# Batch 2's keys: cast by their loads and turned by DMA instead of by the matrix engine

## The chip, the cores and the metric

The kernel runs on one core of a Trainium2 chip. The metric is the device time of one execution in microseconds (us); the kernel before takes 355.89 us (median of 3 runs, 355.85 to 356.45). Five engines with queues of their own work beside each other: PE (TensorE, matrix products; its weight loads have a row PEld), DVE (VectorE), ACT (ScalarE), POOL (GpSimd) and SP (SyncE, which here only starts transfers). ACT and POOL start transfers too. Each engine takes its instructions in the order of the program and waits where data or a buffer is missing.

## What is computed

Causal attention with a decay bias, and a gated feed-forward block on its result:

```python
scores = scale * np.matmul(q, k.transpose(0, 1, 3, 2))        # 8 batches, 8 heads, 576 x 64
s_pos = np.maximum(s, 0.0)
cum = np.cumsum(s_pos, axis=-1)
bias = -(cum[:, :, :, None] - cum[:, :, None, :])
scores = np.where(causal, -1000000000.0, scores + np.minimum(bias, 0.0))
attn = softmax(scores)
x = np.matmul(attn, v).transpose(0, 2, 1, 3).reshape(4608, 512)
xn = x / rms(x) * rms_g
g = xn @ w_gate
out = (g * sigmoid(g) * (xn @ w_val)) @ w_out                 # 512 -> 1536 -> 512
```

## The kernel before

**Two jobs woven into one.** The feed-forward block runs over nine chunks of 512 tokens (`ffn(c)`, line 936). A chunk has 12 pairs of a gate group (line 946, four matmuls of 512 columns) and a value group (line 955, four more), and then four blocks of output matmuls (line 972). Between such groups `step()` (line 851) puts in what the attention needs next. A call of `step` is a slot; a chunk has 36 slots, 24 beside the gate and value groups and 12 beside the output blocks. Slot 0 is the start of chunk 0, so chunk 1 begins behind slot 36, slot 44 follows the fourth value group of chunk 1, slot 45 its fifth gate group. What `step` may put in a slot is decided while the program is written out, by counts of slots (`ready(lag, ...)`), not by time. The order of each engine's queue is fixed by it.

**How queries and keys reach PE.** The scores need queries and keys with the head's elements along the partitions, so each is cast from fp32 to bf16 (`kqn`) and turned (`kqT`). Three constants say which way a batch goes: from batch `XB = 2` on the queries are turned by DMA; from batch `KB = 3` on the keys are cast by the load itself (`load_k`, line 168, one transfer on POOL's queue for each of five blocks of rows) and turned by DMA; from batch `MB = 3` on the scores are computed in a wider form (`s_run`). `kq_dma` (line 178) starts one turning transfer on SP's queue, for one of five column blocks c of the queries (w = 1) or of the keys (w = 0); `x_seq` lists those to come, and a slot starts at most one, at least two slots behind the last.

**Batch 2 before the change.** Its queries come that way. Its keys are loaded in fp32 to `kq32` by ACT's queue (`load2(ACT, 0)`, slot 24, 1 MB and a tail of 128 KB), cast in five pieces on ACT (three) and POOL (two) in slots 36 to 38, turned by PE in four steps of four matmuls (`t_step`, line 199, slots 40 to 43) and a tail of four (`tail_step`, line 222, slot 56), each step read out of the matrix engine's memory by ACT (lines 211 and 235). The queries' five casts lie on ACT (two) and POOL (three) in slots 33 to 36, and their five turns start in slots 37, 39, 42, 44 and 46.

**What uses them.** `s_step(2, kb, g)` (line 257) computes the scores of key block kb for half g of the heads. It needs the keys' block kb and the queries' blocks kb and kb + 1. `av_step` multiplies the softmax weights with the values; x is scaled (`x_scale`, line 481, DVE) and turned to `xnT` by DMA (`xt_dma`, line 489, SP) or, for some blocks, by PE (`xt_step`, line 499).

**Checks.** `check` (line 573) puts on DVE, for every batch's queries and keys, one pass that takes magnitudes (`check_mag`, line 515) and two that keep a running maximum (`check_max`, line 520); their sum decides at the end whether the fast path was allowed.

Of the kernel before, what the change touches and what calls it, by code (L numbers as in the profile page):

```python
# [26 lines left out]
def kernel(  # L27
# [12 lines left out]
    nc = tc.nc  # L40
    B, H, S, D = q.shape
    DM = H * D
# [4 lines left out]
    NSC = 5  # L47
# [33 lines left out]
    kqTn = kqT.rearrange("d a w (h n) -> d a w h n", h=HP)  # L81
    kqTx = kqT.rearrange("d a w (c h n) -> d a w c h n", c=NSC, h=HP)
    XB = 2
    KB = 3
    MB = 3
    PERIOD, PACE, MLAG, XLAG, SQLAG = 9, 2, 1, 6, 2
    v_sb = mp.tile([128, 2, NSC, H, NV], BF16, name="v_sb")
# [437 lines left out]


    SLOTS = 36
    K2 = 33
    slot = [0]
    first, chunk = [0], [0]  # L530
    done = {}
# [17 lines left out]
    x_seq = []  # L549
# [5 lines left out]
    def ready(lag, *key):  # L555
        return at(*key) + lag <= slot[0]
# [16 lines left out]
    def check(b, ws=(1, 0)):  # L573
        t = slot[0] + (8 if b >= KB else 0)

        def when(w):
            if b < 2:
                return slot[0] % 2 and chunk[0] == b and slot[0] > 16
            return phase() >= 25 and slot[0] >= t and (w == 0 or ready(0, "cast", b, 1))
        dve_side.extend((lambda w=w: when(w), f) for w in (ws if b < KB else (0, 1)) for f in (  # L580
            lambda w=w: check_mag(b, w), lambda: check_max(0), lambda: check_max(1),
            lambda w=w: done.__setitem__(("check", b, w), slot[0]))[slice(None) if b < MB - 1 else slice(0, 2)]
            + (() if b < MB - 1 else (lambda w=w: (check_max(1), done.__setitem__(("check", b, w), slot[0])),)))
# [5 lines left out]
    def loads(b, w, when, lag):  # L589

        def main():
            load_kq(nc.scalar, b, w)
            last["L"] = slot[0]
            last["P"] = slot[0] + 2

        def tail():
            load_kq_tail(nc.scalar, b, w)
            done["raw", b, w] = last["L"] = slot[0]
        n = len(act_side)
        when(act_side, lag, [main, tail])  # L600
        act_side[n:] = [(lambda c=c: c() and slot[0] - last["L"] >= 3, f) for c, f in act_side[n:]]

    def casts(b):

        def key(c):
            load_k(b, c)
            last["P"] = slot[0]
            done["K", b, c] = slot[0]  # L610
            if c == NSC - 1:
                check(b)

        def over(w):
            done["cast", b, w] = slot[0]
            if w == 1 and b >= KB:
                if b + 2 < B:
                    loads(b + 2, 1, early, 28 if b <= KB + 1 else 4)
            elif b + 1 < KB or w == 1:
                loads(b + 1, w, early, 11 if (b, w) == (2, 0) else 4)  # L620
            else:
                loads(b + 2, 1, early, 12)
            if w == 1:
                x_seq.extend((b, ww, c) for c in range(NSC) for ww in ((1, 0) if b >= KB else (1,)))
            else:
                done["cast", b] = slot[0]
                check(b)

        def free(w):
            return ready(0, "check", b - 2, w) and (  # L630
                ready(0, "T", b - 2) if w == 0 and b < KB + 2 else
                b < XB + 2 or ready(4, "X", b - 2, w, 4))
        if b > 4:
            key_side.extend((lambda: free(0) and (slot[0] > 72 if b == KB + 1 else ready(0, "R", b - 2, 3) and slot[0] > 3 * SLOTS + 1) and slot[0] - last["P"] >= PACE, lambda c=c: key(c)) for c in range(NSC))
        fns = [(1, lambda r=r: cast_x(nc.gpsimd, b, 1, r)) for r in range(NSC)]
        if b == 2:
            fns[-1] = (1, lambda: (cast_x(nc.gpsimd, b, 1, NSC - 1), over(1)))
        else:
            fns += [(1, lambda: over(1))]
        if b > 4:  # L640
            act_cast.extend((lambda: ready(7, "raw", b, 1) and free(1), f) for f in
                            [lambda r=r: cast_x(nc.scalar, b, 1, r) for r in range(NSC)] + [lambda: over(1)])
            return
        if b < KB:
            fns += [(0, lambda r=r: cast(nc.gpsimd, b, 0, r, r + 1)) for r in range(NSC)]
            fns += [(0, lambda: over(0))]
        if b == 2:

            def put2(queue, t, *fs):
                queue.extend((lambda: slot[0] >= t and free(0) and free(1), f) for f in fs)  # L650
            put2(act_side, K2, *[lambda r=r: cast_x(nc.scalar, b, 1, r) for r in (3, 4)])
            put2(act_side, K2 + 3, *[lambda r=r: cast(nc.scalar, b, 0, r, r + 1) for r in (0, 1, 2)])
            put2(pool_side, K2, *[lambda r=r: cast_x(nc.gpsimd, b, 1, r) for r in (0, 1)],
                 lambda: (cast_x(nc.gpsimd, b, 1, 2), over(1)),
                 lambda: cast(nc.gpsimd, b, 0, 3, 4), lambda: (cast(nc.gpsimd, b, 0, 4, 5), over(0)))
            return
        pool_side.extend((lambda w=w: ready(7, "raw", b, w) and free(w) and (b < 4 or slot[0] > 67), f) for w, f in fns)
        if b <= 4 and b >= KB:
            key_side.extend((lambda c=c: free(0) and slot[0] > (44 if c < 2 else (b - 1) * SLOTS - 3) and slot[0] - last["P"] >= PACE, lambda c=c: key(c)) for c in range(NSC))
# [60 lines left out]

    def soon(b, qb):

        return (b, qb) == (KB, 2)

    def sq_lag(b, qb):
        return 1 if soon(b, qb) else SQLAG
# [42 lines left out]
        return (ready(2, "cast", b) or ready(2, "cast", b, w)) and (b < 2 or ready(1, "S", b - 2, 4, 0))  # L769

    def period(b):
        return 8 if b == KB else PERIOD

    def run_ready():
        if not s_seq or s_seq[0][0] < MB:
# [8 lines left out]
    def can_s():  # L784
        if not s_seq:
            return False
        b, kb, g = s_seq[0]
        if not slot_free(1 if b < MB else 2) or exp_q:
            return False
        if b >= MB:  # L790
            if slot[0] - last["S"] < 3 or slot[0] - last["run"] < period(b) or slot[0] - max(last[x] for x in ("AVT", "TT")) < 2:
                return False
            return run_ready()
        if b == 1 and (phase() < 24 and phase() % 2 == 0 or kb == 4 and at("AV", 1, 3, 1) > slot[0]):
            return False
        due = SLOTS * ((b * S + kb * 128) // DM) - (26 if b == 1 else 15 if b == 2 else 14)
        if slot[0] - last["S"] < (4 if slot[0] < due - 24 else 3 if slot[0] < due else 2):
            return False
        if b >= XB:
            return all(ready(5, "X", b, 1, c) for c in (kb, min(kb + 1, 4))) and (  # L800
                ready(5, "X", b, 0, kb) if b >= KB else ready(3, "T", b) if kb >= 3 else
                all(ready(4 if b == 2 else 3, "T", b, hp, 0) for hp in (2 * g, 2 * g + 1)))
        if kb >= 3 and not ready(3, "T", b):
            return False
        if kb == 4:
            return True
        return all(ready(3, "T", b, 2 * g + j, w) for j in (0, 1) for w in (0, 1))
# [43 lines left out]
    def step(bare=False, tanh=False):  # L851
# [11 lines left out]
        moved = False  # L863
        if scaled[0] < len(x_list):
            b, qb = x_list[scaled[0]]
            if ready(5 if (b, qb) == (1, 1) else (3 if soon(b, qb) else 5 if b == KB else XLAG) if b >= MB else 3, "AV", b, qb, 1):
                x_scale(b, qb)
                last["XS"] = slot[0]
                scaled[0] += 1
                if not by_pe(b, qb):  # L870
                    assert xt_seq[0] == (b, qb)
                    xt_dma(*xt_seq.pop(0))
                    done["XT", b, qb] = slot[0] + 4
                    moved = True
# [4 lines left out]
        if not moved and x_seq and slot[0] - last["X"] >= 2 and not (  # L879
                scaled[0] < len(x_list) and x_list[scaled[0]] != (1, 4) and ready(1 if x_list[scaled[0]][0] < MB else XLAG - 2, "AV", *x_list[scaled[0]], 1)):  # L880
            b, w, c = x_seq[0]
            old = ("R", b - 2, c) if b - 2 >= (XB if w else KB) else ("S", b - 2, 4, 0)
            if (ready(1 if b == 2 else 2, "cast", b, 1) and ready(1, *old)
                    and (w == 1 or ready(7, "K", b, c))):
                x_seq.pop(0)
                kq_dma(b, w, c)
                done["X", b, w, c] = last["X"] = slot[0]
                if b >= KB and (w, c) == (0, NSC - 1) and b + 2 < B:
                    casts(b + 2)
# [176 lines left out]
    with tc.manual_schedule():  # L1066
# [155 lines left out]
        def put(queue, n, *fns):  # L1222
            queue.extend((lambda: slot[0] >= n, f) for f in fns)
# [12 lines left out]
        put(v_side, 11, lambda: (load_wout(0), load_wout(6)))  # L1236
        later(v_side, 0, [
            lambda: load_v(1, 2), lambda: load_v(1, 3), lambda: load_v(1, 4), lambda: load2(POOL, 1)])
        put(act_side, 24, lambda: load2(ACT, 0))
        put(act_side, 30, lambda: nc.scalar.activation(out=vwx, in_=biasK[:, :, MB * H:BH], func=AF.Exp))  # L1240

        check(0, (0,))
# [202 lines left out]
```

## Time and profile before

| | |
|---|---|
| time, median of 3 runs | 355.89 us |
| time of the profiled execution | 355.58 us |
| its span on the core | 354.1 us |
| granted clock of TensorE | 0.999 |
| start of chunk 0, chunk 1, chunk 2 | 26.44, 67.26, 105.24 us |

Times in the views count from the start of the span; the profiled execution has 1.5 us outside it. A row of a timeline gives its start, how long it took, the engine (SPq and ACTq are queues that start transfers), the line of the kernel, the operation with output and inputs, the shape, and a count where like instructions in a row are merged. Matmuls overlap, so that what a group of them costs is read from the start of the next group, not from the duration in the row. In brackets stands the idle time before and what ended it.

### The profile page before, as it was taken

To read this page: it belongs to the slowest core of one execution; us is meant where nothing else is said; L and a number is where in the kernel's file an instruction comes from. 1 tells how busy PE (TensorE), PEld (TensorE's weight loads), DVE (VectorE), ACT (ScalarE), POOL (GpSimd) and SP (SyncE) were. 2 spreads that over 40 slices of the span, in tenths; PEclk is the share of its full clock that TensorE was granted. 3 is DMA by queue.
4 is the path that set the end of the run, shared out by engine and by line. 5 is a ranking of instruction groups with operands and counts; after the bars stand their busy time and mean duration, and the time that the engine had idled before them with its cause. 6 is when DMAs were issued, how large, how long until landed. Compare 5 with 4: busy or idle time off the path is not lost.

```text
span 354.1 us, 6889 instructions
## 1 busy us (share of the span) xinstructions
PE 340.6 (96%) x2374; PEld 165.3 (47%) x2419; DVE 276.9 (78%) x524; ACT 213.4 (60%) x471; POOL 204.5 (58%) x337
## 2 busy tenths in 40 slices
PE   5989999999999999999999999999999999999995
PEld 2445444544444444444554454444544554444443
DVE  6697989598967887798889887988798659836840
ACT  3988885878786546855677557654565445224321
POOL 6969754456769986687597987597745310000000
PEclk9999999999999999999999999999999999999999
DMA  7999999999969998999899999495510121020002
GB/s 220 142 213 270 180 175 259 181 211 181 98 123 177 146 179 118 233 141 202 143 170 105 117 131 185 46 113 90 143 29 17 57 94 23 0 91 30 0 34 93
DMA packets 130528, 45.68 MB, mean 129 GB/s; under 512 B 110548, under 2 KB 125656, under 8 KB 130488
## 3 DMA queue, kind: packets, MB, share of 16 engines
q0 software_dynamic: 67056, 13.70, 50.5%
q1 hardware_dynamic: 53792, 24.20, 33.3%
q10 hardware_dynamic: 9640, 7.29, 8.2%
q8 instruction: 20, 0.33, 0.4%
q14 instruction: 20, 0.16, 0.2%
HBM read 37.90 MB, written 9.44 MB: 134 GB/s over the span
## 4 chain that ended last, share of the span: by engine, by line
PE 77%; DVE 8%; POOL 4%; issue 4%; DMA 3%; ACT 2%; SPq 0%; DVEq 0%; POOLq 0%; ACTq 0%
PE psF L972 25%; PE psF L955 21%; PE psF L946 20%; DVE U L958 2%; PE psAV L443 2%; DMA kq<-in_q_dram 2%; DMA kqT<-kqn 2%; PE psS L286 2%; DVE Ht L951 1%; PE psAV L437 1%; DVE x_sb L453 1%; PE psF L367 1%; POOL v_sb L409 1%; POOL v_sb L194 1%; PE psS L367 1%
## 5 line engine op out<-in xcount | busy, mean ns | idle before, releaser
L955 PE MATMUL psF<-xnT,wv_sb 128*128 128x512 bf16 x424 | 109.9, 379 | 0.4
L946 PE MATMUL psF<-xnT,wg_sb 128*128 128x512 bf16 x414 | 109.0, 379 | 1.3 <-ACT xnT L511 0.3
L949 ACT ACTIVATE T<-psF 128x512 f32<-128x512 f32 x108 | 64.6, 598 | 62.9 <-PE psF L946 58.8
L972 PE MATMUL psF<-wout_sb,Ht 128*128 128x512 bf16 (+2 forms) x428 | 98.9, 373 | 1.4 <-issue 0.8
L958 DVE SCALAR_TENSOR_TENSOR U<-T,psF 128x512 bf16<-128x512 f32 x108 | 73.7, 682 | 24.1 <-ACT T L949 23.9
L951 DVE TENSOR_TENSOR Ht<-U,psF 128x512 bf16<-128x512 bf16 x99 | 67.8, 685 | 6.9
L972 PEld LDWEIGHTS <-Ht 128*128 128x128 bf16 x444 | 40.1, 98 | 43.5 <-issue 1.4
L955 PEld LDWEIGHTS <-wv_sb 128*128 128x128 bf16 x432 | 39.6, 98 | 44.5 <-issue 2.9
L946 PEld LDWEIGHTS <-wg_sb 128*128 128x128 bf16 x432 | 39.4, 98 | 42.9 <-issue 2.4
L976 ACT ACTIVATE osb<-psF 128x512 f32<-128x512 f32 (+2 forms) x37 | 21.7, 587 | 58.4 <-PE psF L972 50.8
L384 POOL TENSOR_SCALAR_AFFINE_SELECT E<-E 128x512 bf16<-128x512 bf16 (+1 forms) x50 | 34.8, 704 | 28.5 <-ACT E L380 18.7
L194 POOL DMA_DIRECT2D v_sb<-in_v_dram x40 | 35.3, 885 | 0.2 <-issue 0.2
L484 DVE SCALAR_TENSOR_TENSOR xs_sb<-x_sb,al_all,g_row 128x512 bf16<-128x512 bf16 (+1 forms) x36 | 29.6, 823 | 4.1 <-POOL al_all L477 3.9
L474 POOL TENSOR_SCALAR al_all<-ss_all 128x1 f32<-128x1 f32 (+2 forms) x39 | 11.5, 295 | 35.9 <-ACT xs_sb L461 27.9
L310 ACT ACTIVATE E<-psS,biasK 128x256 bf16<-128x256 f32 (+3 forms) x88 | 29.2, 426 | 2.6 <-PE psS L286 2.6
L453 DVE TENSOR_TENSOR x_sb<-psAV,rZ 128x256 bf16<-128x256 f32 (+1 forms) x66 | 28.0, 424 | 2.3
L522 DVE TENSOR_TENSOR acc<-acc,mag 128x1280 bf16<-128x1280 bf16 x32 | 27.3, 873 | 0.2
L477 POOL TENSOR_TENSOR al_all<-al_all,mhalf 128x1 f32<-128x1 f32 (+2 forms) x39 | 25.2, 645 | 3.2
L443 PEld LDWEIGHTS <-E 128*128 128x128 bf16 x320 | 21.7, 97 | 10.5 <-POOL E L384 0.7
L461 ACT ACTIVATE xs_sb<-x_sb 128x512 bf16<-128x512 bf16 (+1 forms) x37 | 23.3, 629 | 4.6 <-DVE x_sb L453 4.0
L409 POOL TENSOR_TENSOR v_sb<-v_sb,vwx 128x512 bf16<-128x512 bf16 x25 | 25.9, 1037 | 0.1
L443 PE MATMUL psAV<-v_sb,E 128*128 128x65 bf16 x264 | 23.8, 193 | 0.1
(136 smaller groups left out, 379.8 us busy)
## 6 DMA issues: line engine op xcount, KB each, us to landing
out_dram<-osb SPq DMA_DIRECT2D x35, 256.0 KB, 2.7
kq<-in_q_dram ACTq DMA_DIRECT2D x5, 1024.0 KB, 7.5
v_sb<-in_v_dram POOLq DMA_DIRECT2D x32, 128.0 KB, 4.9
kqn<-in_k_dram POOLq DMA_DIRECT2D x20, 128.0 KB, 5.1
kq<-in_k_dram SPq DMA_DIRECT2D x4, 512.0 KB, 5.8
kq<-in_q_dram SPq DMA_DIRECT2D x4, 512.0 KB, 7.5
wout_sb<-in_moe_w_out_dram POOLq DMA_DIRECT2D x2, 768.0 KB, 10.5
kq<-in_q_dram POOLq DMA_DIRECT2D x1, 1024.0 KB, 11.0
```

Source lines behind the costliest of these rows:

```text
L194: nc.gpsimd.dma_start(out=v_sb[0:n, b % 2, c, :, 0:64], in_=v[b, :, c * 128:c * 128 + n, :].rearrange("h p d -> p h d"))
L384: nc.gpsimd.affine_select(out=Ev, in_=Ev, pattern=[[0, 4], [1, nq]], compare_op=ALU.is_ge, fill=0.0, base=0, channel_multiplier=-1)
L409: nc.gpsimd.tensor_tensor(out=v_sb[:, b % 2, c, :, 0:64], in0=v_sb[:, b % 2, c, :, 0:64], in1=vwx[:, c, i:i + H].unsqueeze(2).to_broadcast ...
L443: nc.tensor.matmul(o, lhsT=d, rhs=v_sb[:, p, qb, h, :], start=(j == 0 and qb == 0), stop=(j == 3))
L453: nc.vector.tensor_tensor(out=xo[:, g * 256:(g + 1) * 256].rearrange("p (h d) -> p h d", h=4), in0=pv[R, :, 0:64], in1=rZ[R].unsqueeze(2). ...
L484: nc.vector.scalar_tensor_tensor(out=xs_sb[R, (b * NSC + qb) % NX, :], in0=x_sb[R, (b * NSC + qb) % NX, :], scalar=al_all[R, col:col + 1], ...
L946: nc.tensor.matmul(Gp, lhsT=wg_sb[:, cc, fs], rhs=xnT[:, cc, x0:x0 + DM], start=(cc == 0), stop=(cc == CC - 1))
L949: nc.scalar.activation(out=T, in_=Gp, func=AF.Tanh, scale=0.5)
L951: nc.vector.tensor_tensor(out=Ht[:, fb - 1, :], in0=pend[0], in1=pend[1], op=ALU.mult)
L955: nc.tensor.matmul(Vp, lhsT=wv_sb[:, cc, fs], rhs=xnT[:, cc, x0:x0 + DM], start=(cc == 0), stop=(cc == CC - 1))
L958: nc.vector.scalar_tensor_tensor(out=U, in0=T, scalar=1.0, in1=Gp, op0=ALU.add, op1=ALU.mult)
L972: nc.tensor.matmul(Op[:, p0:p1], lhsT=Ht[:, fb, tb * 128:(tb + 1) * 128], rhs=wout_sb[:, fb, p0:p1], start=(fb == 0), stop=(fb == FB - 1))
```

## The change

The constant `KB` goes from 3 to 2. With it batch 2's keys are loaded and cast by POOL's queue in five transfers (slots 24, 26, 36, 43 and 45, by the list `K0`) and turned by five DMA transfers on SP (slots 33, 35, 44, 50 and 56). The fp32 load of the keys on ACT's queue, their five casts, PE's 20 transposing matmuls and the five copies out of the matrix engine's memory fall away. Of the queries' casts three now lie on ACT and two on POOL. `x_seq` for batch 2 is written out by hand, keys and queries mixed. The queries' turns start in slots 37, 39, 42, 46 and 52 instead of 37, 39, 42, 44 and 46. The scores of batch 2 start in slot 44 instead of 45, and several of its later steps one or two slots earlier. The checks of batch 1's queries start in slot 35, at the end of chunk 0, instead of slot 37. Conditions that named `KB` for what begins at batch 3 now name `MB`. From slot 73 on both programs have the same order.

```diff
-    KB = 3
+    KB = 2
...
-    K2 = 33
+    K2, K0 = 33, (24, 26, 36, 39, 42)
...
             if b < 2:
-                return slot[0] % 2 and chunk[0] == b and slot[0] > 16
+                return slot[0] % 2 and (16 < slot[0] < SLOTS if b == 0 else slot[0] > 34 and slot[0] - last["XS"] > 1)
...
             if w == 1 and b >= KB:
+                if b == KB:
+                    loads(3, 1, early, 4)
                 if b + 2 < B:
-                    loads(b + 2, 1, early, 28 if b <= KB + 1 else 4)
-            elif b + 1 < KB or w == 1:
-                loads(b + 1, w, early, 11 if (b, w) == (2, 0) else 4)
-            else:
-                loads(b + 2, 1, early, 12)
-            if w == 1:
+                    loads(b + 2, 1, early, 14 if b == KB else 28 if b <= KB + 2 else 4)
+            elif b + 1 < KB:
+                loads(b + 1, w, early, 4)
+            if w == 1 and b > 2:
                 x_seq.extend((b, ww, c) for c in range(NSC) for ww in ((1, 0) if b >= KB else (1,)))
-            else:
+            elif w == 0:
                 done["cast", b] = slot[0]
                 check(b)
...
-            put2(act_side, K2, *[lambda r=r: cast_x(nc.scalar, b, 1, r) for r in (3, 4)])
-            put2(act_side, K2 + 3, *[lambda r=r: cast(nc.scalar, b, 0, r, r + 1) for r in (0, 1, 2)])
-            put2(pool_side, K2, *[lambda r=r: cast_x(nc.gpsimd, b, 1, r) for r in (0, 1)],
-                 lambda: (cast_x(nc.gpsimd, b, 1, 2), over(1)),
-                 lambda: cast(nc.gpsimd, b, 0, 3, 4), lambda: (cast(nc.gpsimd, b, 0, 4, 5), over(0)))
+            put2(act_side, K2, *[lambda r=r: cast_x(nc.scalar, b, 1, r) for r in (3, 4)],
+                 lambda: (cast_x(nc.scalar, b, 1, 2), over(1)))
+            put2(pool_side, K2, *[lambda r=r: cast_x(nc.gpsimd, b, 1, r) for r in (0, 1)])
+            key_side.extend((lambda c=c: free(0) and slot[0] >= K0[c] and slot[0] - last["P"] >= PACE, lambda c=c: key(c)) for c in range(NSC))
+            x_seq.extend([(2, 0, 0), (2, 0, 1), (2, 1, 0), (2, 1, 1), (2, 1, 2), (2, 0, 2), (2, 1, 3), (2, 0, 3), (2, 1, 4), (2, 0, 4)])
             return
...
-        return (b, qb) == (KB, 2)
+        return (b, qb) == (MB, 2)
...
-        return 8 if b == KB else PERIOD
+        return 8 if b == MB else PERIOD
...
-        due = SLOTS * ((b * S + kb * 128) // DM) - (26 if b == 1 else 15 if b == 2 else 14)
+        due = SLOTS * ((b * S + kb * 128) // DM) - (26 if b == 1 else 13 if (b, kb) == (2, 2) else 15 if b == 2 else 14)
...
-            if ready(5 if (b, qb) == (1, 1) else (3 if soon(b, qb) else 5 if b == KB else XLAG) if b >= MB else 3, "AV", b, qb, 1):
+            if ready(5 if (b, qb) == (1, 1) else (3 if soon(b, qb) else 5 if b == MB else XLAG) if b >= MB else 3, "AV", b, qb, 1):
...
-            if (ready(1 if b == 2 else 2, "cast", b, 1) and ready(1, *old)
+            if ((ready(1, "cast", b, 1) or w == 0) if b == 2 else ready(2, "cast", b, 1)) and (ready(1, *old)
                     and (w == 1 or ready(7, "K", b, c))):
...
-        put(act_side, 24, lambda: load2(ACT, 0))
```

## The prediction

> **What bounds the kernel now.** First the top of the profile's page, then what PE waited for from 26 us, where the chunks begin, to 130 us (second fence) and from there to the end (third).
>
> ```profile
> span 354.1 us, 6889 instructions
> PE 340.6 (96%) x2374; PEld 165.3 (47%) x2419; DVE 276.9 (78%) x524; ACT 213.4 (60%) x471; POOL 204.5 (58%) x337
> ```
> ```profile
> PE psF L946 <- ACT xnT L511: 0.3, 1, 0.3
> ```
> ```profile
> PE psF L972 <- issue: 0.8, 5, 0.2
> ```
>
> PE is busy for 96% of the span, and behind 26 us it waits 0.3 + 0.8 = 1.1 us in all. So the time is the sum of what PE is given: one us less of matmuls is one us less of time, and one us of new waiting is one more. ACT and POOL have 40% of the span free; their work counts only where it makes something late for PE.
>
> **What PE no longer does.** Below are rows of PE's timeline in chunk 1, the first and the last of the four transposing steps of batch 2's keys and what stands around them, and then the tail.
>
> ```profile
> 70.96 0.39 PE L203 MATMUL psAV<-ident_bf,kqn 128*128 128x128 bf16 x4
> 71.18 1.03 PE L946 MATMUL psF<-xnT,wg_sb 128*128 128x512 bf16 x3
> ...
> 74.22 0.39 PE L203 MATMUL psAV<-ident_bf,kqn 128*128 128x128 bf16 x4
> 74.44 1.03 PE L955 MATMUL psF<-xnT,wv_sb 128*128 128x512 bf16 x4
> 75.30 1.03 PE L946 MATMUL psF<-xnT,wg_sb 128*128 128x512 bf16 x4
> 76.26 0.39 PE L286 MATMUL psS<-kqT 64*128 64x256 bf16 x4
> ...
> 81.34 0.29 PE L443 MATMUL psAV<-v_sb,E 128*128 128x65 bf16 x4
> 81.47 1.02 PE L946 MATMUL psF<-xnT,wg_sb 128*128 128x512 bf16 x4
> 82.43 0.39 PE L286 MATMUL psS<-kqT 64*128 64x256 bf16 x4
> ```
> ```profile
> 87.88 0.39 PE L228 MATMUL psT<-ident_bf,kqn 128*128 128x128 bf16 x4
> 88.10 1.03 PE L946 MATMUL psF<-xnT,wg_sb 128*128 128x512 bf16 x3
> ```
>
> A step's row says 0.39 us, but the next group starts 71.18 - 70.96 = 0.22 us later, and it is starts that add up on a full engine. Four steps are 4 x 0.22 = 0.89 us with the last digits (0.22 to 0.23 each), the tail 88.10 - 87.88 = 0.22 us: 1.11 us together. No matmul is added, and the scores' matmuls read the turned keys as 128 columns in a row as before. So the first term is -1.11 us.
>
> [...]
>
> **What is off the path.** ACT loses four copies out of the matrix engine's memory, the tail's copy and three key casts and gains one query cast; POOL loses three casts and gains five starts of loads. ACT is only relieved by this, so it costs nothing there; the loads' row and landings are:
>
> ```profile
> L170 POOL DMA_DIRECT2D kqn<-in_k_dram x25: 692/895/1107, 87.4 to 215.2; - x25
> DMA to landing us min/median/max: 3.4/5.3/8.0
> ```
>
> The next rows are POOL's around the first two key loads, PE's turn of x's block 2, and DVE's.
>
> ```profile
> 58.84 0.19 POOL L474 TENSOR_SCALAR al_all<-ss_all 128x1 f32<-128x1 f32 x1 [3.33 <-DVE rZ L451]
> ...
> 59.62 0.64 POOL L319 TENSOR_SCALAR_AFFINE_SELECT E<-E 128x512 bf16<-128x512 bf16 x1
> 60.69 0.19 POOL L474 TENSOR_SCALAR al_all<-ss_all 128x1 f32<-128x1 f32 x1 [0.43 <-ACT xs_sb L461]
> 60.97 0.55 POOL L477 TENSOR_TENSOR al_all<-al_all,mhalf 128x1 f32<-128x1 f32 x1
> ...
> 72.14 2.73 POOL L194 DMA_DIRECT2D v_sb<-in_v_dram  x3
> ```
> ```profile
> 63.12 0.39 PE L504 MATMUL psT<-ident_bf,xs_sb 128*128 128x128 bf16 x4
> ```
> ```profile
> 61.82 0.74 DVE L484 SCALAR_TENSOR_TENSOR xs_sb<-x_sb,al_all,g_row 128x512 bf16<-128x512 bf16 x1
> ...
> 67.46 0.18 DVE L451 RECIPROCAL rZ<-psAV 64x4 f32<-64x4 f32 x1 [1.54 <-PE psAV L443]
> 67.67 0.42 DVE L453 TENSOR_TENSOR x_sb<-psAV,rZ 64x256 bf16<-64x256 f32 x1
> 68.02 0.81 DVE L516 TENSOR_SCALAR mag<-kqn 128x2560 uint16<-128x2560 uint16 x1
> ```
>
> Load 0 (0.9 us) starts in the 3.33 us that POOL stood idle before 58.84. Load 1 stands behind the mask at 59.62, runs from 60.26 to 61.16 (61.37 by the longest start), and pushes the scaling factor behind it from 61.52 to about 62.0 to 62.2. DVE scales x then until 62.85 to 63.05, and PE turns it at 63.12: cover of 0.07 to 0.27 us, so I take nothing; were it gone, PE would wait what is missing, some tenths. Loads 2 to 4 stand where POOL casts less or before the values' loads finish; what waits behind them are masks that the weights' products need some five slots later. The moved check (0.81 us) fits into DVE's 1.54 us idle before 67.46. The loads replace 1 MB in rows of 1 KB by four times as many of 256 bytes, but land in 5.3 us (8.0 at most) and have seven slots, about 7 us, before their turn.
>
> **What PE may now wait for.** This is the term that decides. The scores of block 0 (76.26 before) need the queries' column block 1; those of block 1 (82.43 before) need column block 2. SP's rows, and the landings of these two turns and of all:
>
> ```profile
> 62.12 6.11 SPq L977 DMA_DIRECT2D out_dram<-osb  x3
> 68.33 2.55 SPq L190 DMA_TRANSPOSE kqT<-kqn  x2
> 73.61 1.17 SPq L495 DMA_TRANSPOSE xnT<-xs_sb  x1
> 74.87 3.90 SPq L190 DMA_TRANSPOSE kqT<-kqn  x3
> ```
> ```profile
> L190 SPq DMA_TRANSPOSE kqT<-kqn x1: 1230/1230/1230, 69.6 to 69.6; - x1
> DMA to landing us min/median/max: 4.8/4.8/4.8
> ```
> ```profile
> L190 SPq DMA_TRANSPOSE kqT<-kqn x1: 1230/1230/1230, 74.9 to 74.9; - x1
> DMA to landing us min/median/max: 5.9/5.9/5.9
> ```
> ```profile
> L190 SPq DMA_TRANSPOSE kqT<-kqn x55: 1169/1230/2202, 68.3 to 255.4; - x55
> DMA to landing us min/median/max: 2.3/4.0/7.6
> ```
>
> Block 1 landed at 69.6 + 4.8 = 74.4, 1.9 us before its use; block 2 at 74.87 + 5.9 = 80.8, 1.7 us before. After the change the scores of block 0 stand one slot earlier and 0.89 us of steps ahead of them are gone: PE is there at 75.30 - 0.89 = 74.41. The second is there at 81.34 + 0.13 (the product that moves ahead of it, 81.47 - 81.34) - 0.89 = 80.6. Both come out within 0.2 us of the landing: all of the slack is spent. What sets the landings hardly moves. SP's two key turns (1.23 us each) go into the 6.11 us in which it starts only three stores and else waits, ahead of the last store; x's turn at 73.61 waits for the same chain of ACT, POOL and DVE as before. SP works in order, though: key turn 1 waits for load 1, due at 60.26 + 5.3 = 65.6 when SP comes to it at about 66.6. At 8.0 us it would be there at 68.3, the last store and the queries' turns behind it 1.6 us late, and the first scores too. So with unchanged landings the waiting is 80.8 - 80.6 = 0.2 us in all, since a wait at the first only makes PE later at the second. Its bounds are 0 (transfers land as the median of 4.0 us) and 74.87 + 7.6 - 80.6 = 1.9 us (the longest of 55). How full the DMA engines are is in the share behind the clock:
>
> ```profile
> 67.00:69.00 2.00, 2.00 (x18) 1.04 (x17) 1.37 (x4) 1.73 (x4) 0.93 (x2) 1.00 0.28 108
> 71.00:75.00 4.00, 3.95 (x31) 2.32 (x31) 3.81 (x6) 3.24 (x6) 3.76 (x5) 1.00 0.94 269
> 75.00:79.00 4.00, 4.00 (x23) 1.60 (x20) 3.77 (x6) 3.15 (x8) 0.50 (x1) 1.00 2.01 166
> ```
>
> Key load 2 and the first two key turns fall where the share is 0.28 of 1; load 3 starts at 72.14 + 2.73 = 74.87 behind the values' loads, no earlier than block 2's turn. So I take 0.2 us, near the lower end.
>
> **The sum.** -1.11 + 0.2 = -0.9 us on the profiled execution's 355.58 us (span 354.1 and 1.5 around it): 354.7. The median of the runs lies 0.3 us above that execution, so the forecast is 355.89 - 0.9 = 355.0.
>
> **The rivals.** A measurement of this kernel can tell about 0.2%, 0.71 us: faster is below 355.18, slower above 356.60.
>
> *The gain goes into the wait.* If the landings slip by 1 us, the waiting is 1.2 us and the time 355.89 - 1.11 + 1.2 = 356.0. For it speaks that both scores now come within 0.2 us of their data; against it that the added transfers mostly stand later in the queues.
>
> *DVE becomes the pace.* It is busy 3.81 of the 4 us from 71 to 75. If it held chunk 1, only the moved check's 0.81 us less the 0.6 us of a product's read-out that comes into the chunk, 0.2 us, would be won: 355.7. Against it: the check leaves just before DVE is tightest, and PE waited for DVE nowhere.
>
> *The other side: block 2 gets caught in the traffic.* From 75 to 79 us the share is 2.01, more asked than served. Load 3, load 4, the key turns and the next 1 MB of queries come into that stretch earlier or anew. At the longest landing, 7.6 us, PE waits 1.9 us: 355.89 - 1.11 + 1.9 = 356.7. It decides the sign from 1.1 us of waiting, and the verdict "slower" from 1.8 us. [...] The landings here came nearly in the order of starts, so I hold it for the less likely.
>
> **Chances.** Forecast 0.52; the gain used up 0.20 and DVE as the pace 0.05; the other side 0.17, and 0.06 for a long wait that I don't see. So faster 0.52, same 0.25, slower 0.23. The forecast's own range is 354.6 to 355.2; up to the other cases it is 354.6 (no wait, less 0.2 for the measurement) to 356.7 (the longest landing).
>
> **What would show it.** Right: chunk 1 takes some 37.1 us instead of 105.24 - 67.26 = 37.98; no rows of line 203 behind 60 us; at most a few tenths of waiting of line 286 for kqT. Wrong: line 286, or a group behind it, waiting a us or more for a turn by DMA; SP's turns of the queries starting later than 68.3 and 74.9; PE waiting for DVE or for xnT at a chunk's start.

## The result and the profile after

The changed kernel takes 360.38 us (median of 6 runs, 358.63 to 363.91) against 355.94 for the kernel before beside it (6 runs, 355.71 to 356.45): a ratio of 1.0133, interval 1.0084 to 1.0183. It is slower, by 1.3%. The profiled execution took 359.58 us. Times here and below leave out slow executions, those over 1.5% above the fastest of the same kernel: one each of the runs with the key load sooner, with the load two slots later (its profiled one) and with key 1 behind. The top of the changed kernel's page, and what PE waited for from 26 to 130 us and from there to the end:

```profile
span 358.1 us, 6856 instructions
PE 340.0 (95%) x2354; PEld 164.2 (46%) x2399; DVE 277.9 (78%) x524; ACT 209.7 (59%) x464; POOL 209.8 (59%) x339
```
```profile
PE psS L286 <- DMA kqT<-kqn: 3.0, 1, 3.0
PE psF L946 <- DVE Ht L951: 0.6, 1, 0.6
PE psF L946 <- ACT xnT L511: 0.3, 1, 0.3
```
```profile
PE psF L972 <- issue: 0.8, 5, 0.2
PE psF L367 <- DMA kqT<-kqn: 0.5, 1, 0.5
```

PE has its 20 matmuls fewer (2354 for 2374), and three waits that were not there before: 3.0 us for a turn of batch 2 (kqT), 0.6 us for VectorE (Ht) and 0.5 us for another turn. Where the span grew shows from the first gate matmul (line 946) of each chunk:

| | before chunk 0 | chunk 0 | 1 | 2 | 3 | 4 to 7 | 8 |
|---|---|---|---|---|---|---|---|
| before | 26.44 | 40.82 | 37.98 | 37.11 | 36.52 | 139.68 | 35.54 |
| after | 27.23 | 40.81 | 39.86 | 37.93 | 36.90 | 139.68 | 35.67 |
| difference | +0.79 | 0 | +1.88 | +0.82 | +0.38 | 0 | +0.13 |

Chunk 1 grew by the 3.0 us wait less the 1.1 us of removed turns. Chunks 2 and 3 hold the two other waits; chunk 3 also differs by 0.2 us between two profiles of the kernel before (36.52 and 36.32). PE's rows around the long one, at the first scores of batch 2:

```profile
74.32 1.03 PE L955 MATMUL psF<-xnT,wv_sb 128*128 128x512 bf16 x4
78.33 0.39 PE L286 MATMUL psS<-kqT 64*128 64x256 bf16 x4 [2.98 <-DMA kqT<-kqn]
78.66 1.04 PE L946 MATMUL psF<-xnT,wg_sb 128*128 128x512 bf16 x4
```

PE stands 2.98 us for a turn by DMA. SP's rows say which one:

```profile
66.24 2.52 SPq L190 DMA_TRANSPOSE kqT<-kqn  x2
68.86 0.54 SPq L977 DMA_DIRECT2D out_dram<-osb  x1
69.49 2.55 SPq L190 DMA_TRANSPOSE kqT<-kqn  x2
74.38 1.17 SPq L495 DMA_TRANSPOSE xnT<-xs_sb  x1
75.65 1.23 SPq L190 DMA_TRANSPOSE kqT<-kqn  x1
```
```profile
L190 SPq DMA_TRANSPOSE kqT<-kqn x2: 1222/1247/1272, 69.5 to 70.8; - x2
...
DMA to landing us min/median/max: 3.5/5.5/7.4
```

The pair at 66.24 are the new key turns. Behind them stand the last store of chunk 0 and the queries' blocks 0 (69.49) and 1 (70.8). In the kernel before, with chunk 1 starting at 67.26 instead of 68.04, the same store and the same two blocks were:

```profile
67.89 0.33 SPq L977 DMA_DIRECT2D out_dram<-osb  x1
68.33 2.55 SPq L190 DMA_TRANSPOSE kqT<-kqn  x2
```

Block 1 landed 7.4 us after its issue, at 78.2; before it took 4.8. Next to it on ACT's queue goes batch 3's 1 MB query load, in the changed kernel (first fence) and in the one before (second):

```profile
70.99 0.63 ACT L461 ACTIVATE xs_sb<-x_sb 64x512 bf16<-64x512 bf16 x1 [1.29 <-DVE x_sb L453]
71.08 0.41 ACTq L137 DMA_DIRECT2D kq<-in_q_dram  x1
```
```profile
70.38 0.37 ACTq L137 DMA_DIRECT2D kq<-in_q_dram  x1
```

The load starts 71.08 - 70.76 = 0.32 us behind block 1's turn now and started 70.38 - 69.64 = 0.74 us behind it before. What the queues moved in the changed kernel from 72.5 to 77.5 us (q10 is ACT's, q1 SP's, q0 POOL's):

```profile
q10 hardware_dynamic: 1506, 1.17, 98.9%
q1 hardware_dynamic: 323, 0.07, 10.4%
q0 software_dynamic: 26, 0.00, 1.7%
```

The packets of ACT's queue, where this load stands, took 98.9% of the DMA engines' time in the stretch in which block 1's turn is under way; SP's queue moved 323 packets beside it.

### The profile page after: what moved, and what is told of

It is laid out like the page before. It is cut to its first block, busy times and chain, and to the rows that moved or that the text cites. A ratio compares the mean times of both kernels' runs of the same rounds, so it can differ in the third digit from the quotient of the medians.

```text
span 358.1 us, 6856 instructions
## 1 busy us (share of the span) xinstructions
PE 340.0 (95%) x2354; PEld 164.2 (46%) x2399; DVE 277.9 (78%) x524; ACT 209.7 (59%) x464; POOL 209.8 (59%) x339
## 4 chain that ended last, share of the span: by engine, by line
PE 78%; DMA 5%; DVE 5%; POOL 4%; issue 4%; ACT 2%; SPq 1%; DVEq 0%; POOLq 0%; ACTq 0%
PE psF L972 25%; PE psF L955 20%; PE psF L946 20%; DMA kqT<-kqn 4%; PE psAV L443 2%; PE psS L286 2%; DMA kq<-in_k_dram 2%; PE psAV L437 2%; PE psF L367 1%; DVE U L958 1%; POOL v_sb L409 1%; DVE x_sb L453 1%; PE psS L367 1%; DVE xs_sb L484 1%; DVE Ht L951 1%
## 5 line engine op out<-in xcount | busy, mean ns | idle before, releaser
L972 PE MATMUL psF<-wout_sb,Ht 128*128 128x512 bf16 (+2 forms) x428 | 98.9, 373 | 1.4 <-issue 0.8
L958 DVE SCALAR_TENSOR_TENSOR U<-T,psF 128x512 bf16<-128x512 f32 x108 | 73.6, 682 | 26.7 <-ACT T L949 26.4
L484 DVE SCALAR_TENSOR_TENSOR xs_sb<-x_sb,al_all,g_row 128x512 bf16<-128x512 bf16 (+1 forms) x36 | 30.5, 847 | 4.7 <-POOL al_all L477 4.6
L170 POOL DMA_DIRECT2D kqn<-in_k_dram x30 | 26.9, 898 | 0.6 <-issue 0.3
L477 POOL TENSOR_TENSOR al_all<-al_all,mhalf 128x1 f32<-128x1 f32 (+2 forms) x39 | 25.1, 643 | 3.2
```

What stands on the lines that cost most here:

```text
L484: nc.vector.scalar_tensor_tensor(out=xs_sb[R, (b * NSC + qb) % NX, :], in0=x_sb[R, (b * NSC + qb) % NX, :], scalar=al_all[R, col:col + 1], ...
L958: nc.vector.scalar_tensor_tensor(out=U, in0=T, scalar=1.0, in1=Gp, op0=ALU.add, op1=ALU.mult)
L972: nc.tensor.matmul(Op[:, p0:p1], lhsT=Ht[:, fb, tb * 128:(tb + 1) * 128], rhs=wout_sb[:, fb, p0:p1], start=(fb == 0), stop=(fb == FB - 1))
```

## Experiments

Times are medians; the ratio is to the kernel before, run beside each. Chunk lengths are read as above.

**What holds the turn up: the load, or the new key load beside it?** Theory A blames the 1 MB load, theory B the third key load (slot 36). Four edits of the changed kernel:

```diff
-                    loads(3, 1, early, 4)
+                    loads(3, 1, early, 10)
```


> The changed kernel with the 1 MB load of batch 3's queries started in slot 45 instead of 39; the casts that need it come up to 7 slots later. Theory A (this load, started 0.3 us behind the turn of the queries' block 1, holds that turn up): block 1 lands within 4 us, the first scores wait less than 0.3 us, and the time is 354.8 to 356. Theory B (the third key load, in slot 36, pushes block 1's turn back): block 1 still takes over 6 us and the first scores wait 1 us or more; 357 or more.

```diff
-    K2, K0 = 33, (24, 26, 36, 39, 42)
+    K2, K0 = 33, (24, 26, 28, 39, 42)
```


> The changed kernel with the third key load started in slot 28 instead of 36, nothing else moved. Theory B: block 1 lands within 5 us, as before the change, the first scores wait 0.5 us at most, the time is 354.8 to 356. Theory A: the 1 MB load still comes 0.3 us behind block 1's turn, the landing stays over 6.5 us, the wait over 2 us, the time over 358.

```diff
-            load_kq(nc.scalar, b, w)
+            if (b, w) != (3, 1):
+                load_kq(nc.scalar, b, w)
```


> The changed kernel without the 1 MB load of batch 3's queries (its 512 main rows are left out, so batch 3's result is another one). Theory A: no wait for a turn in chunk 1, 354.5 to 355.3. Theory B: block 1 lands over 5 us after its start and the first scores wait about 1 us; 356.

```diff
-            load_k(b, c)
+            if (b, c) != (2, 2):
+                load_k(b, c)
```


> The changed kernel without the third key load (batch 2's keys 256 to 383 are left out, so batch 2's result is another one). Theory B: block 1 lands within 5 us, wait 0.5 us at most, 354.8 to 356. Theory A: landing over 6.5 us, wait over 2 us, over 358.

Without the load (its 512 rows of batch 3's queries are not fetched): 356.74 us, 1.0015 [0.9996, 1.0035]. Block 1 landed 2.9 us after its issue. PE's waits of that run:

```profile
PE psF L947 <- DVE Ht L952: 0.6, 1, 0.6
PE psS L286 <- DMA kqT<-kqn: 0.6, 1, 0.6
```

The 0.6 us for kqT is at the second scores. Chunk 1 took 37.47 us = 37.98 - 1.11 + 0.6, so the term of the turns is there in full. The time is above the 354.5 to 355.3 that theory A gave, by this wait and by chunk 2 (37.94). Moving or leaving out the key load gave 360.26 (1.0132 [1.005, 1.0213]) and 360.43 (1.0106 [1.0061, 1.015]), with 2.5 and 2.1 us still waited at the first scores. B falls. The load six slots later freed block 1 too (2.9 us, no wait there), but batch 3's casts and turns hang on it, and PE waited elsewhere, 6.6 us at one place: 375.76, 1.0547 [1.0496, 1.0598]. This late a load costs more than it frees.

**Why now and not before: the gap.** Theory C: the second key turn holds SP, so that the last store comes 0.2 us and the queries' turns 0.3 to 0.4 us later, and the load follows block 1 at 0.3 us instead of 0.74. (The other 0.2 us is the store's own start, which held SP for 0.54 us instead of 0.33.) Two runs move the load, by one slot and by two; two let the first turns stand in neighbouring slots, the second with the load two slots later:

```diff
-            load_kq(nc.scalar, b, w)
+            after(1, lambda: load_kq(nc.scalar, b, w)) if (b, w) == (3, 1) else load_kq(nc.scalar, b, w)
```


> The changed kernel with one instruction moved: batch 3's 1 MB query load is issued one slot (about 1 us) later, slot 40 for 39; every other instruction keeps its slot. Theory C (what holds block 1's turn up is how soon the load follows it: 0.32 us behind it in the changed kernel, 0.74 us in the one before, because two key turns of 1.2 us each now stand ahead of block 1 on SyncE's queue): the load starts at least 1 us behind block 1's turn, block 1 lands within 4.8 us of its issue instead of 7.4, and the 3.0 us wait at the first scores of batch 2 shrinks below 0.5. The same load is then still in front of block 2's turn, which landed 7.7 us after its issue; PE gets to the second scores some 3 us sooner than in the changed kernel, so 2 to 3.5 us of waiting appear there and the time stays at 358.5 to 360. Theory D (the bytes of the load slow the turns wherever it stands in this stretch): block 1 still needs over 6 us and the first wait stays at 2 us or more.

> The same move by two slots (slot 41), all else in its slot. Theory C: block 1 lands within 3.5 us of its issue and the first scores wait less than 0.3 us; block 2's turn, issued 2 to 3 us behind the load, meets it whole and lands 8 us or more after its issue, so the second scores wait 2.5 to 4.5 us: 358.5 to 361. Theory D: the first wait stays at 2 us or more.

```diff
+    EARLY = ((2, 0, 1), (2, 1, 0), (2, 1, 1), (2, 1, 2))
...
+        if b == 2 and slot[0] < 44:
+            return False
...
-        if not moved and x_seq and slot[0] - last["X"] >= 2 and not (
+        if not moved and x_seq and slot[0] - last["X"] >= (1 if x_seq[0] in EARLY else 2) and not (
```


> The changed kernel with the turns of key block 1 and of query blocks 0, 1 and 2 of batch 2 allowed in neighbouring slots instead of every second one (slots 34, 36, 37, 38 for 35, 37, 39, 42), the first scores held at slot 44 where they are in the changed kernel, and the 1 MB load at its slot 39. Theory C: block 1's turn is issued 0.7 to 1 us ahead of the load and lands within 5 us, before PE is there; block 2's turn is issued about when the load is, so it needs some 7 us, but from 71 us instead of 75.7, and lands by 79 us, ahead of the second scores: no wait over 0.3 us at either. Chunk 1 takes 36.9 to 37.5 us and the kernel 355.2 to 356.6. Theory D: both blocks still land 6 us or more behind their issue and the kernel stays above 358.

> The run before with the 1 MB load also moved by two slots (to slot 41), so that all three query turns that the first and second scores need are issued ahead of it. Theory C: blocks 1 and 2 land within 4 us of their issue, no wait at the first or second scores, chunk 1 36.9 to 37.3 us, the kernel 355.0 to 356.3; batch 3's casts, whose slots stay, may wait up to 1 us for the later load, off PE's path. Theory D: above 357.5.

One slot: 361.11 (1.0133 [1.0089, 1.0176]). A miss of the edit: ACT stands waiting for DVE in front of both slots (the 1.29 us in the row at 70.99), so the load still started 0.31 us behind the turn and block 1 needed 6.9 us. Close turns: 360.99 (1.013 [1.0109, 1.0152]), a miss too: SP worked for 1.2 us on each turn, so block 1 left at 70.78, as in the changed kernel, 0.29 us ahead of the load. Two slots: 361.02 (1.0125 [1.0083, 1.0167]); in its profile block 1 landed in 2.8 us, nothing was waited at the first scores, and 1.9 us at the second. Both edits: 358.41 (1.0076 [1.0052, 1.01]); block 1 left 2.09 us ahead of the load:

```profile
L190 SPq DMA_TRANSPOSE kqT<-kqn x1: 1271/1271/1271, 70.8 to 70.8; - x1
...
DMA to landing us min/median/max: 3.0/3.0/3.0
```

No scores waited there. So a load that stands in this stretch does not slow the turn wherever it stands (theory D): 2 us behind it, it cost nothing. The time still missed the 355.0 to 356.3 that C gave: PE waited 0.6 us for values (v_sb) in chunk 1, and the 0.6 us waits of chunks 2 and 3 were there too. Now the order of the turns, key block 1 behind the queries' blocks 0 and 1 (the first scores held at slot 44 as above):

```diff
-            x_seq.extend([(2, 0, 0), (2, 0, 1), (2, 1, 0), (2, 1, 1), (2, 1, 2), (2, 0, 2), (2, 1, 3), (2, 0, 3), (2, 1, 4), (2, 0, 4)])
+            x_seq.extend([(2, 0, 0), (2, 1, 0), (2, 1, 1), (2, 0, 1), (2, 1, 2), (2, 0, 2), (2, 1, 3), (2, 0, 3), (2, 1, 4), (2, 0, 4)])
```


> The changed kernel with the turn of key block 1 of batch 2 placed behind those of query blocks 0 and 1 on SyncE (turns in slots 33, 36, 38, 40 for key 0, query 0, query 1, key 1), the first scores held at slot 44, and the 1 MB load at its slot 39. Theory C (one key turn of 1.2 us ahead of query block 1 on SyncE is what lets the load catch it): block 1's turn is issued 1 us or more ahead of the load, lands within 4 us, and the first scores wait less than 0.3 us instead of 3.0. Key block 1 and query block 2 are now the ones beside the load, 7 to 8 us each, so the second scores, which PE reaches some 3 us sooner, wait 2 to 3.5 us: 358.3 to 360. If the key turns do not matter, the first wait stays above 2 us.

359.39, 1.0086 [1.0055, 1.0116]. Store and block 1 went out 0.63 and 2.39 us behind the start of chunk 1, as in the kernel before (0.63 and 2.38), so the second key turn is what had shifted them. Block 1 got 0.65 us ahead of the load, not a full one, and its landing and wait, then all waits for kqT at line 286:

```profile
  PE psS L286: 0.6, 1
...
DMA to landing us min/median/max: 5.4/5.4/5.4
```
```profile
PE psS L286 <- DMA kqT<-kqn: 2.6, 2, 2.0
```

The first wait fell from 3.0 to 0.6 us, and 2.0 us came up at the second scores, as expected: block 2's turn, issued 4.9 us behind the load, needed 8.1 us there, 7.7 in the changed kernel and 5.9 before. Without the 1 MB load it needed 6.3, so most of the difference goes with that load as well. The converse, in the kernel before, with no key turn and no key load of the change (the load's start in slot 40 falls away):

```diff
-                 lambda: cast(nc.gpsimd, b, 0, 3, 4), lambda: (cast(nc.gpsimd, b, 0, 4, 5), over(0)))
+                 lambda: cast(nc.gpsimd, b, 0, 3, 4), lambda: (cast(nc.gpsimd, b, 0, 4, 5), over(0), load_kq(nc.scalar, 3, 1)))
```


> The kernel before (keys of batch 2 turned by PE, no key turn and no key load by cast at all) with one instruction moved: batch 3's 1 MB query load is issued behind the last key cast of slot 38 instead of in slot 40, so that ScalarE no longer waits for VectorE in front of it; it should start 0.3 to 1 us sooner than 70.4, within 0.4 us of the turn of query block 1 at 69.6, before or behind it. If the gap between the two is the cause (theory C), that turn lands 6.3 to 8.4 us behind its issue instead of 4.75, which uses up its 1.9 us of slack: the first scores wait 0 to 2 us for it and the kernel takes 356.2 to 358.2. If the key turns or key loads are needed for the loss, the turn still lands within 5 us and the time stays at 355.9.

356.31, 1.0012 [0.9991, 1.0033]. The load started at 70.17, 0.37 us behind the turn:

```profile
L190 SPq DMA_TRANSPOSE kqT<-kqn x1: 1230/1230/1230, 69.8 to 69.8; - x1
...
DMA to landing us min/median/max: 6.6/6.6/6.6
```

It landed at 76.4, PE came at 76.6: all but 0.2 of the 1.9 us of slack is gone without any key turn. The gaps side by side (the changed kernel's own order ran in several of these kernels):

| run | load behind the turn, us | turn landed after, us |
|---|---|---|
| close turns | 0.29 | 7.3 |
| load one slot later | 0.31 | 6.9 |
| key load 2 sooner; left out; old checks | 0.30 | 7.0; 6.6; 8.4 |
| changed kernel | 0.32 | 7.4 |
| before, load sooner | 0.37 | 6.6 |
| key 1 behind | 0.65 | 5.4 |
| before | 0.74 | 4.8 |
| close turns, load two slots later | 2.09 | 3.0 |
| no load | - | 2.9 |

The order is clear, the landing at one gap is not exact: at 0.30 us it lies between 6.6 and 8.4 us.

**The 0.6 us in chunk 2.** VectorE's first scale of x there and the two casts beside it on GpSimd, of the changed kernel (two fences) and of the kernel before (two more):

```profile
111.41 1.57 DVE L484 SCALAR_TENSOR_TENSOR xs_sb<-x_sb,al_all,g_row 128x512 bf16<-128x512 bf16 x1
```
```profile
111.81 0.62 POOL L164 CAST kqn<-kq 128x512 bf16<-128x512 f32 x1
112.36 1.09 POOL L153 CAST kqn<-kq 128x512 bf16<-128x512 f32 x1
```
```profile
108.75 0.75 DVE L484 SCALAR_TENSOR_TENSOR xs_sb<-x_sb,al_all,g_row 128x512 bf16<-128x512 bf16 x1
```
```profile
109.16 0.80 POOL L164 CAST kqn<-kq 128x512 bf16<-128x512 f32 x1
109.91 0.60 POOL L153 CAST kqn<-kq 128x512 bf16<-128x512 f32 x1
```

Theory E: the scale doubles because the casts run beside it. They were moved:

```diff
-        fns = [(1, lambda r=r: cast_x(nc.gpsimd, b, 1, r)) for r in range(NSC)]
+        fns = [(1, lambda r=r: after(3, lambda: cast_x(nc.gpsimd, b, 1, r)) if (b, r) in ((4, 3), (4, 4)) else
+                cast_x(nc.gpsimd, b, 1, r)) for r in range(NSC)]
```


> The changed kernel with the last two casts of batch 4's queries on GpSimd issued three slots later (76 and 77 for 73 and 74), so that they no longer stand beside the 128x512 scale of x on VectorE at the start of chunk 2. Theory E (this scale took 1.57 us in the changed kernel and 0.75 us in the one before because two casts on GpSimd ran beside it): the scale takes 0.8 us or less, PE's 0.6 us wait for Ht at the start of chunk 2 is gone and chunk 2 takes 37.1 to 37.3 us instead of 37.9; the first scores still wait 2.5 to 3 us, so the kernel stays at 358.3 to 361. The rival (the shift of batch 2's scores and AV steps by a slot makes VectorE late) keeps the wait and chunk 2 at 37.9 us.

```profile
110.93 0.79 DVE L484 SCALAR_TENSOR_TENSOR xs_sb<-x_sb,al_all,g_row 128x512 bf16<-128x512 bf16 x1
```
```profile
PE psS L286 <- DMA kqT<-kqn: 2.5, 1, 2.5
PE psF L947 <- ACT xnT L511: 0.3, 1, 0.3
```

The scale takes 0.79 us, the wait for Ht is gone, chunk 2 takes 37.17 us, and the wait at the scores stays: 359.88, 1.0096 [1.0066, 1.0126]. E holds as far as this: without the casts beside it the scale does not double. In the kernel before it has the same neighbours and does not double either, so something more is needed.

**The load in another place.** In slot 24 its buffer stands empty since the change (its starts in slots 39 and 42 fall away); then the same with close turns and later casts, and that with the load in slot 30:

```diff
+        put(act_side, 24, lambda: (load_kq(nc.scalar, 3, 1), load_kq_tail(nc.scalar, 3, 1)))
```


> The changed kernel with batch 3's 1 MB query load and its tail issued in slot 24 of chunk 0, where the kernel before loaded batch 2's keys (that buffer stands empty there since the change), all else in its slot. Theory C: nothing large is in flight from 71 to 78 us, block 1 lands within 3.5 us of its issue and the first scores do not wait; block 2, issued at 75.6, lands within 6.5 us as in the run without the load, 0 to 0.8 us behind PE. Chunk 1 takes 36.9 to 37.7 us, chunk 2 still 37.9 with its 0.6 us wait for Ht: 355.9 to 357.0. Theory D (the turns are slow in this stretch whatever the load does) keeps it above 358.5. A third way is that the load in chunk 0 delays what chunk 1 starts with, which would show as a chunk 0 longer than 41.0 us.

> Three of these put together: the 1 MB load in slot 24, batch 2's first key and query turns in neighbouring slots (34, 36, 37, 38) with the first scores at slot 44, and batch 4's last two casts three slots later. If C and E are the whole loss, neither scores of batch 2 nor chunk 2 wait any more, chunk 1 takes 36.8 to 37.2 us, chunk 2 37.1 to 37.3, and the 1.1 us of the removed transposes remain: 354.6 to 355.4. If some loss is left that neither names, it is 355.8 or more.

> As the run of three edits together, with the 1 MB load in slot 30 instead of 24, behind the turn of x (issued at 61.6) whose landing chunk 1 waited for there. If the collision with that turn was the rest of the loss, it lands by 67 us, chunk 0 takes 40.8 to 41.1 us instead of 42.1, chunk 1 36.8 to 37.1, chunk 2 37.2: the kernel takes 355.0 to 355.9, about what the kernel before takes. If the load only moves the loss on, to the key turns or to the first scores, it is 356.5 or more.

Slot 24 alone: 358.38, 1.0051 [1.0031, 1.007], above what was expected. Block 1 landed in 2.8 us and chunk 1 took 37.37 us, as C has it, but chunk 0 took 41.31, the third way. The three edits: 357.38, 1.0032 [1.0011, 1.0054], with chunk 0 at 42.08, a wait of 0.7 us for a turn of x at the start of chunk 1, which took 37.36, and chunk 2 at 37.15. The three edits were to give 354.6 to 355.4 if C and E were the whole loss; the longer chunk 0 is what they cost. With slot 30 it got worse, 359.6, 1.0083 [1.0053, 1.0113], chunk 0 43.90, chunk 1 38.47 (of which some 1.6 us are a halved clock, below): the load went out at 61.63, 0.2 us behind the turn of x at 61.4 that chunk 1 starts with:

```profile
L495 SPq DMA_TRANSPOSE xnT<-xs_sb x1: 2250/2250/2250, 61.4 to 61.4; - x1
...
  PE psF L952: 2.3, 1
...
DMA to landing us min/median/max: 9.4/9.4/9.4
```

In the changed kernel this turn landed in 4.2 us. The expectation had put the load safely "behind" the turn; just behind it was the worst place of those tried.

**The turns alone, the checks, the kernel before again.** The kernel before without the 20 transposes and their copies (the tail's step is left out in the same way); the changed kernel with the old times of the checks; the kernel before once more:

```diff
     def t_step(b, hp, w, pT=None, dve=None):
+        if b == 2:
+            return
```


> The kernel before without the 20 transposes of batch 2's keys and the copies behind them (batch 2's scores then use batch 0's keys), all else in its slot. My term: chunk 1 is 1.1 us shorter (36.9 for 38.0), the kernel 354.6 to 355.1, unless what follows waits where it did not: the first scores of batch 2 had 0.0 us of slack on query block 1 and the second 0.1 behind PE on block 2, so up to 1 us may come back as waiting for their turns (then 355.5 to 356).

```diff
-                return slot[0] % 2 and (16 < slot[0] < SLOTS if b == 0 else slot[0] > 34 and slot[0] - last["XS"] > 1)
+                return slot[0] % 2 and chunk[0] == b and slot[0] > 16
```


> The changed kernel with batch 1's checks where the kernel before has them (slots 37, 39, 41 for 35, 37, 39). If the checks have no part in the loss, the same 2.4 to 3 us at the first scores and 0.6 us for Ht in chunk 2, and 359 to 361.5. If they have, a wait for VectorE goes and the time is under 358.

> The kernel before, profiled a second time. If the 0.4 us more before chunk 0 and the 0.1 to 0.5 us more in the last chunk are differences between executions, this profile has the first FFN matmul of chunk 0 up to 0.5 us away from 26.44 and a last chunk up to 0.4 us away from 35.54; the chunks between agree to 0.05 us. If they are the change's, both repeat to 0.1 us.

Without the turns: 355.98, 0.9991 [0.9975, 1.0007]. Chunk 1 is 0.57 us shorter (37.41), not 1.1; PE's waits:

```profile
PE psF L950 <- DVE U L962: 0.4, 1, 0.4
PE psF L950 <- ACT xnT L515: 0.3, 1, 0.3
```

A wait for VectorE takes 0.4 of it back; the remaining 0.1 shows as no wait. So the removal alone, with nothing in its place, gives nothing that these runs can tell from none. The old checks: 360.87 (1.0109 [1.0063, 1.0155]) with 3.9 us at the scores and chunk 2 at 37.94, so the moved checks are not what loses the time. The kernel before again: 355.48 us, 26.58 before chunk 0, chunks 1 and 2 37.97 and 37.14, the last 35.45: these repeat to 0.1 us, chunk 3 (36.32 for 36.52) to 0.2.

## Why the prediction failed

**The time.** 355.0 was forecast, with a range up to 356.7; it is 360.4. In the profiled executions the span was to fall by 0.9 us and grew by 4.0. Of these 4.9 us, 2.8 are the wait at the first scores (3.0 us where the sum had 0.2 us in all), 0.8 chunk 2, 0.4 chunk 3, 0.8 the stretch before chunk 0 and 0.1 chunk 8.

**The removed turns.** Right: the run without the load shows the 1.1 us in chunk 1. In the kernel before, with nothing put in their place, they are worth half of it, as VectorE then sets the pace at one point. That is the mechanism of the rival that was given 0.05; in the changed kernel no wait for VectorE shows in chunk 1.

**The costs off the path.** The key loads on POOL and the scaling factors behind them cost PE nothing before chunk 1 (chunk 0 is 40.81 us for 40.82). The moved check cost nothing either.

**The step that failed** is "What sets the landings hardly moves", which gave the first scores no wait: block 1's landing was left at 4.8 us, and it took 7.4. The 1 MB load on ACT's queue, 0.74 us behind that turn, has no place in the sum. Its first wrong premise is that SP's two key turns go "ahead of the last store" and move nothing. By the sum's own 66.6 the second ends at 66.6 + 1.23 = 67.83, 0.06 us before that store's 67.89: there was no room. It ended at 66.24 + 2.52 = 68.76, and against the chunk's start the store left 0.2 us later (68.86 - 68.04 = 0.82 for 67.89 - 67.26 = 0.63) and block 1 0.34 us later (70.76 - 68.04 = 2.72 for 69.64 - 67.26 = 2.38), while the load left when it did (3.04 for 3.12). The sum prices a shift on SP's queue at its own size (1.6 us late, the scores 1.6 us late); 0.34 us cost 2.6 us of landing here, by what stood behind the turn on the other queue. Of its signs of being wrong, turns "starting later than 68.3 and 74.9", the first came true (1.45 us behind the chunk's start for 1.07) and the second did not (7.61 both times).

**The bound.** The longest landing of 55, 7.6 us, was put on the second scores alone, which gave 1.9 us. On the first it gives 69.64 + 7.6 - 74.41 = 2.8, close to the 3.0 measured. That "a wait at the first only makes PE later at the second" was true, and so the second scores waited for nothing; but the larger of the two waits had to be priced. Even so the sum would have come to 355.89 - 1.11 + 2.8 = 357.6 us, short of 360.4.

**The rivals.** The other side had the right mechanism, a turn caught in the traffic, but named block 2, and load 3 first among the transfers that come beside it. Block 2 did land late, 7.7 us after its issue for 5.9, more by the 1 MB load than by load 3 (6.3 without the former); PE, 3 us late itself, did not have to wait for it. The landings came in the order of starts here too (block 1 at 78.2 us, the 1 MB load at 71.08 + 7.4 = 78.5), and still the turn was slowed by a load that started behind it: it landed 7.4 us after its issue, and 2.9 us without the load.

**Not foreseen:** the 0.8 us in chunk 2, the 0.4 us in chunk 3 with a wait for a turn (0 to 1 us of it in most other profiles), and the spread of the times, below. Left open is the 0.8 us before chunk 0, where both programs do the same (the first instruction that differs starts at 53 us): fifteen profiles with the change have 26.8 to 27.3 us there, the four without it 26.4 to 26.7.

## What to carry to other kernels

Here a turn that moved by 0.34 us landed 2.6 us later after its issue (7.4 for 4.8), as a 1 MB load on another queue then followed it at 0.32 us instead of 0.74: compare each transfer's issue with the nearest large load's on every queue, before and after, and price its landing by the longest of its kind at every use whose slack the change spends. Time taken off a full engine is only won if the next engine and the next transfer are early enough: here the first two scores were left with 0.0 and -0.2 us of slack by the prediction's own sum, and VectorE alone took back 0.4 of the 1.1 us.

## What the runs showed of the hardware

**Behind waits of 2.1 to 3.9 us PE's granted clock fell to 0.50 in five profiles.** Stretches with the busy time of PE, PEld, DVE, ACT and POOL, and then, third from the end, PE's granted clock (behind it the DMA engines' share and GB/s), first of the run with the old checks, then of the changed kernel:

```profile
74.00:78.00 4.00, 1.13 (x6) 0.29 (x3) 3.79 (x7) 0.60 (x1) 2.30 (x3) 1.00 2.04 246
78.00:82.00 4.00, 2.95 (x10) 1.05 (x11) 0.39 (x1) 1.32 (x3) 0.00 (x0) 0.57 3.42 96
```
```profile
78.00:82.00 4.00, 3.67 (x22) 1.55 (x23) 1.53 (x3) 2.70 (x7) 0.86 (x2) 1.00 2.85 137
```

In the run with the old checks PE stood for 3.9 us until 79.05, and its granted clock was 0.50 from 78.5 to 81.9 (0.57 over the row's 4 us). For the 2.85 us in which it worked there, half the clock is about 1.4 us lost, and chunk 1 took 42.14 = 37.98 - 1.11 + 3.92 + 1.35 us. The profiled execution of the changed kernel kept 1.00 after 3.0 us. The runs with close turns (2.9 us), with the load one slot later (2.4 us), with the load in slot 30 (2.3 us) and without the third key load (2.1 us) had 3.4 us at 0.50 too (mean clock of these four 0.994 to 0.995); those with the casts later and with the key load sooner (2.5 us each) did not (0.999 and 0.998). One such stretch costs an estimated 3.4 / 2 = 1.7 us at most. It goes with the spread of the times: the changed kernel's runs at a mean clock of 0.998 and above took 358.6 to 359.7 us, those at 0.995 361.1 to 363.9, of which 363.9 is more than one stretch explains. What decides it was not shown: a wait of 2.1 us was enough once, and one of 3.0 us was not.

**Two casts on GpSimd doubled an operation on VectorE**, 1.57 for 0.75 us (0.79 with the casts moved later), and in the kernel before the same neighbours left it alone: there the first cast was the one stretched (0.80 for 0.62). All eleven profiles in which the change and those slots were kept have the scale at 1.56 to 1.58 us and chunk 2 at 37.9 to 38.0 us, the four without the change 0.75 and 37.1. What tips it was not settled; GpSimd's operation in front (L477) starts 2.41 to 2.42 us behind the start of chunk 2 in the eleven and 2.45 to 2.46 in the four, and whether these 0.04 us do it was not tested.
